# Two evacuations of stage 1 shared anew, and the drain before the MLP done group by group

**Chip, cores, metric.** One core of one Trainium2 chip. Times are device microseconds (us) of one execution. PE or TensorE multiplies matrices, ACT is ScalarE, DVE is VectorE and POOL is GpSimd.

## The reference, cut to what matters

The input has 2048 rows of 512. Two blocks follow each other, each with a layer norm and a residual:

```python
X  = rfft2(layernorm(x)) * (w_r + 1j * w_i)
h  = x + irfft2(X).astype(bf16)
a  = relu(layernorm(h) @ w1 + b1)
h2 = h + (a * a) @ w2 + b2
```

## The kernel before

The Fourier transforms are matmuls with tables of sines, which the kernel makes itself. It has these parts in time:

- **Stage 1** (to about 20 us): the 16 row groups of x are normalised and multiplied by a table. GpSimd makes the reciprocal roots of the variances (`rs1`), VectorE multiplies the table by them (the folds, `KFr`), TensorE multiplies, ScalarE or VectorE takes the result from PSUM to SBUF (the evacuation, `Bt`).
- **Spectral part** (to about 50 us): nine rounds with the intermediate tiles U, X (or AB, from which VectorE makes X), Z, M and T. `EI` is a table for the inverse transform: TensorE transposes it, ScalarE copies it from PSUM, VectorE negates parts of it (`EN`). `GI` and, with the change, `GIn` are tables of sines for the drain.
- **Drain** (50 to 57 us): the last inverse step for the first two row groups, their residual, second layer norm and transposes. Nothing of the MLP can start before it is through.
- **MLP** (57 us to the end): TensorE is busy; the matmuls into `ph` are its first half. The remaining row groups are drained beside it.

The parts that the change touches, cut:

```python
# stage 1. split=True: two PSUM tiles, evacuated in halves by ScalarE and VectorE
ln1_fold(6, 10)
angles_g(1)                       # two GpSimd instructions
ln1_rstd(10, 14)                  # add and power on GpSimd: the roots of groups 10 to 13
gathers = [w_reversed(0)]         # indirect DMA, made ready by GpSimd
...
nc.gpsimd.tensor_tensor(rs1[:, 14:16], rs1[:, 14:16], mhalf[:, 0:2], ALU.pow)
ln1_fold(12, 14)
gathers.append(w_reversed(1))
ln1_fold(14, 16)
stage1(10, cp=nc.vector.tensor_copy)
...
stage1(12)
tr08 = stage1(14, split=True, pre=lambda o: transposed(o, (0, 8), True))
# spectral rounds
for pr in range(9):
    ...
    if pr == 3:
        table_neg((4, 7))                         # VectorE, reads EI
        ...                                       # EN from EI, VectorE
    ...
    if pr == 1:
        table_neg((1, 3))
        tr = mm_tile("ptr", BF16)
        transposed(tr, (4, 5, 6, 7))              # TensorE
        table_i(tr, (4, 5, 6, 7))                 # ScalarE: EI
    if pr == 5:
        sin_of(GI[:].rearrange("p t c -> p (t c)"), fiI[:])    # ScalarE
# drain. s5: four matmuls into one bank, the odd half copied to od by ScalarE;
# s5b: R from sum and difference, VectorE; s6: matmul by KI; s6a/s6b: residual, statistics
s5(0); s5(1); s5(2, True); s5(3, True)
idle = bank("idle", "ph", 3)
s5b(0); s5b(1)
s6(0); s6b(0, True)
s6(1); s6a(1); s6b(1)
rstd(0); norm(0)
warm(idle[:], 12)                 # matmuls that do nothing but keep TensorE busy
s5b(2)
transp(0, 0); transp(0, 1)
for c in range(5):
    run(c)                        # the MLP
```

Of the kernel before, what the change touches and what calls it, by code (L numbers as in the profile page):

```python
# [34 lines left out]
def kernel(  # L35
# [43 lines left out]
    ones = persist.tile([P, 512], BF16, name="ones")  # L79
    KI = persist.tile([P, P], BF16, name="KI")  # L80
    GI = persist.tile([P, 4, 256], BF16, name="GI")
    T2 = persist.tile([P, 4, G, 16, 8], BF16, name="T2")

    fwd = tc.alloc_tile_pool(name="fwd", bufs=1)
# [34 lines left out]
    def mm_tile(name, dt=FP32):  # L119
        return ps.tile([P, 4096 // mybir.dt.size(dt)], dt, tag="mm", name=name)  # L120

    def sin_of(dst, fi):

        nc.scalar.activation(dst, fi.bitcast(I16)[:, ::2], ACT.Sin, scale=SIN_SCALE)
# [30 lines left out]
    def w_reversed(i):  # L155
        return nc.gpsimd.indirect_dma_start(
            out=WB[i][:, 9:16, :].rearrange("p j l -> p (j l)"), out_offset=None,
            in_=(A_w_r, A_w_i)[i].rearrange("k l -> (k l)").unsqueeze(1), element_offset=9 * Df,
            in_offset=bass.IndirectOffsetOnAxis(ap=idxR[:, 0:1], axis=0))
# [29 lines left out]

    nc.gpsimd.tensor_scalar(cols[:, 0:1], pF[:, 0:1], 128.0, None, ALU.mult)  # L190
    nc.gpsimd.tensor_scalar(cols[:, 1:2], pF[:, 0:1], 128.0, 16384.0, ALU.mult, ALU.add)

    def angles_g(t):
        o = 512 * t
        for r, q in ((0, QT), (256, HT)):
            nc.gpsimd.tensor_scalar(fiG[:, o + r:o + r + 256], idxL[:, r:r + 256], cols[:, t:t + 1], float(q),
                                    ALU.mult, ALU.add)

    def table_e(i):
        nc.scalar.activation(EF[:, :, i, :], fiE[i][:].bitcast(I16)[:, ::2].rearrange("p (a b) -> p a b", a=9),  # L200
# [25 lines left out]
    def ln1_rstd(a, b):  # L226
        nc.gpsimd.tensor_scalar(rs1[:, a:b], mv1[:, a:b, 1], EPS, None, ALU.add)
        nc.gpsimd.tensor_tensor(rs1[:, a:b], rs1[:, a:b], mhalf[:, 0:b - a], ALU.pow)
# [6 lines left out]
    def stage1(g0, n=0, split=False, pre=None, cp=nc.scalar.copy):  # L235
        if split:
            two = [mm_tile("p1a"), mm_tile("p1b")]
            pts = [pt[:, 0:512] for pt in two]
        else:
            pt = mm_tile("p1")  # L240
            pts = [pt[:, 0:512], pt[:, 512:1024]]
        pvs = [o.rearrange("p (e i c) -> p e i c", e=2, i=2) for o in pts]
        warm(pts[0], n)
        if pre:
            pre(two[0][:, 512:1024].bitcast(BF16))
        for t in range(2):
            for i in range(2):
                g = g0 + i
                o = pvs[t][:, :, i, :]
                nc.tensor.matmul(o, lhsT=xs[:, g, P * t:P * t + P],  # L250
                                 rhs=KFr[:, g, 0:P].unsqueeze(1).to_broadcast([P, 2, P]), start=True, stop=False)
                nc.tensor.matmul(o, lhsT=xs[:, g, 256 + P * t:256 + P * t + P],
                                 rhs=KFr[:, g, :].rearrange("p (e c) -> p e c", e=2), start=False, stop=True)
        dst = Bt[:].rearrange("p e q (g s) -> p e g q s", s=8)[:, :, g0:g0 + 2]
        if split:
            for t, cph in ((0, nc.scalar.copy), (1, nc.vector.tensor_copy)):
                cph(dst[:, 2 * t:2 * t + 2], pts[t].rearrange("p (e i q s) -> p e i q s", e=2, i=2, q=16))  # L257
            return two[0][:, 512:1024].bitcast(BF16)
        else:
            cp(dst, pt[:].rearrange("p (e i q s) -> p e i q s", e=4, i=2, q=16))  # L260

    def warm(o, n):

        for _ in range(n):
            nc.tensor.matmul(o, lhsT=ones[:, 0:P], rhs=ones[:], start=True, stop=True)  # L265
# [13 lines left out]
    def table_neg(ks):  # L279
        nc.vector.tensor_scalar(EI[:, ks[0]:ks[-1] + 1, 2, :], EI[:, ks[0]:ks[-1] + 1, 0, :], -1.0, None, ALU.mult)  # L280
# [29 lines left out]
    table_c(slice(0, 9, 8))  # L310
    ln1_stats(10, 12)
    ln1_fold(6, 10)
    angles_g(1)
    ln1_rstd(10, 14)
    gathers = [w_reversed(0)]
    stage1(6, 2)
    sin_of(GF[:].rearrange("p t c -> p (t c)"), fiG[:])
# [6 lines left out]
    ln1_fold(12, 14)  # L324
    gathers.append(w_reversed(1))
    ln1_fold(14, 16)
    stage1(10, cp=nc.vector.tensor_copy)
    for k, (dst, src) in enumerate(((W1[:], B_w1.rearrange("(c p) f -> p c f", p=P)),
                                    (W2[:], B_w2.rearrange("(i p) d -> p i d", p=P)),
                                    (b1b[:], B_b1.rearrange("(i p) -> p i", p=P)),  # L330
# [2 lines left out]
        if k == 0:  # L333
            for ga in gathers:
                after(load, ga, "the rows of W first")
    stage1(12)

    nc.vector.tensor_scalar(GF[:, :, 255:256], GF[:, :, 255:256], 0.5, None, ALU.mult)
    nc.vector.tensor_scalar(EF[:, :, 2, :], EF[:, :, 0, :], -1.0, None, ALU.mult)
# [169 lines left out]
    for pr in range(9):  # L509
        if pr == 1:  # L510
            stage3(3)
        if pr + 3 < 8:
            stage2(pr + 3)
        if pr == 0:
            tr = mm_tile("ptr", BF16)
            transposed(tr, (1, 2, 3))
            table_i(tr, (1, 2, 3))
        if 1 < pr and pr + 2 < 8:
            stage3(pr + 2)
        if pr == 7:  # L520
            warm(mm_tile("idle")[:, 0:512], 3)
        if pr > 0:
            stage4(pr - 1, split=(pr == 8))
        if pr == 8:
            warm(mm_tile("idle")[:, 0:512], 3)
        if pr == 3:
            table_neg((4, 7))
            nc.vector.tensor_scalar(EN[:].rearrange("p n (k b) -> p n k b", k=2), EI[:, NO_M[0]:NO_M[-1] + 1, 0:2, :],
                                    -1.0, None, ALU.mult)
        if pr == 0:  # L530
            spectral(0, first_tables)
        elif pr < 8:
            spectral(pr)
        if pr == 1:
            table_neg((1, 3))
            tr = mm_tile("ptr", BF16)
            transposed(tr, (4, 5, 6, 7))
            table_i(tr, (4, 5, 6, 7))
        if pr == 5:
            sin_of(GI[:].rearrange("p t c -> p (t c)"), fiI[:])  # L540
            nc.gpsimd.tensor_copy(b1f[:], b1b[:])
        if pr == 6:
            nc.scalar.activation(junk1[:], eps[:], ACT.Sqrt, bias=eps[:])
# [19 lines left out]
    def s5(g, ahead=False):  # L563
        pe = bank("p5", "po", 2) if ahead else bank("p5", "pp", 3)
        for e in range(2):
            for r in range(2):
                lt = 2 * r + e
                nc.tensor.matmul(pe[:, 256 - 256 * e:512 - 256 * e], lhsT=T2[:, lt, g].rearrange("p q s -> p (q s)"),  # L568
                                 rhs=GI[:, lt, :], start=(r == 0), stop=(r == 1))
        od = ffn.tile([P, 256], FP32, tag="od", bufs=4, name="od")  # L570
        nc.scalar.copy(od[:], pe[:, 256:512])  # L571
        Rs[g] = pe, od

    def s5b(g):
        pe, od = Rs[g]
        Rs[g] = R = ffn.tile([P, 512], BF16, tag="R", bufs=3, name="R")
        nc.vector.tensor_tensor(R[:, 0:256], pe[:, 0:256], od[:], ALU.add)  # L577
        nc.vector.tensor_tensor(R[:, 256:512], pe[:, 0:256], od[:], ALU.subtract)

    def s6(g):  # L580
        py = bank("p6", "pp", 3)
        if g == 0:
            nc.tensor.matmul(py[:], lhsT=identW[:], rhs=xs[:, 0, :], start=True, stop=False)
            nc.tensor.matmul(py[:], lhsT=KI[:], rhs=Rs.pop(g)[:], start=False, stop=True)
            nc.scalar.activation(hs[:, 0, :], py[:], ACT.Copy, scale=WSC, accum_out=mv2[:, 0, 0:1])
            return
        nc.tensor.matmul(py[:], lhsT=KI[:], rhs=Rs.pop(g)[:], start=True, stop=True)  # L587
        Ys[g] = py

    def s6a(g):  # L590
        nc.vector.scalar_tensor_tensor(hs[:, g, :], Ys.pop(g)[:], WSC, xs[:, g, :], ALU.mult, ALU.add)  # L591
# [20 lines left out]
    def rstd(c):  # L612
        a, b = CHUNKS[c]
        for par in range(2):
            mine = [g for g in range(a, b) if on_act(c, g) != bool(par)]
            if mine:
                st = mine[1] - mine[0] if len(mine) > 1 else 1
                sl = slice(mine[0], mine[-1] + 1, st)
                nc.scalar.activation(sd2[:, sl], mv2[:, sl, 1], ACT.Sqrt, bias=eps[:], scale=1.0 if par else float(D) ** -3 if c == 0 else 1.0 / D)
        if c == 0:  # L620
            nc.vector.tensor_scalar(mv2[:, 0, 0:1], mv2[:, 0, 0:1], 1.0 / D, None, ALU.mult)
        nc.vector.reciprocal(rs2[:, a:b], sd2[:, a:b])
# [4 lines left out]
    def norm(c):  # L627
        a, b = CHUNKS[c]
        us[c] = u2 = ffn.tile([P, 4, D], BF16, tag="u2", bufs=2, name="u2")
        for g in range(a, b):  # L630
            nc.vector.tensor_scalar(u2[:, g - a, :], hs[:, g, :], mv2[:, g, 0:1], rs2[:, g:g + 1],
                                    ALU.subtract, ALU.mult)
# [114 lines left out]
                piece()  # L747
                at += cost

    s5(0)  # L750
    s5(1)
    s5(2, True)
    s5(3, True)
    idle = bank("idle", "ph", 3)
    s5b(0)
    s5b(1)
    s6(0)
    s6b(0, True)
    s6(1)
    s6a(1)  # L760
    s6b(1)
    rstd(0)
    norm(0)
    warm(idle[:], 12)
    s5b(2)
    transp(0, 0)
    transp(0, 1)
    for c in range(5):
        run(c)
    pin(tc, nc)  # L770
# [30 lines left out]
```

## Time and profile before

| | before |
|---|---|
| time, median | 173.03 us |
| profiled span | 171.1 us |
| TensorE busy | 92% of the span |
| last evacuation of stage 1 starts (`Bt` from `p1b`) | 19.71 us |
| last T evacuation ends (the spectral part's end) | 49.92 us |
| group 1's matmul by `KI` starts | 52.70 us |
| first matmul into `ph` starts | 57.13 us |

A line of a timeline or of the chain has the start in us from the beginning of the span, the duration in us, the engine and what it did; a timeline adds the idle time before it and, behind an arrow, what ended that. TensorE is busy for 92% of the span, yet the part before 57 us is set by waits of one engine for another. The lines themselves are in the prediction.

### The profile page before, as it was taken

How to read it: one execution, taken by the hardware profiler on the slowest of the kernel's cores; microseconds unless marked ns; L12 is line 12 of the kernel's file. 1: busy time of each engine (PE TensorE's matmuls, PEld its weight loads, DVE VectorE, ACT ScalarE, POOL GpSimd, SP SyncE). 2: the span in 40 equal slices, each digit the busy share in tenths (PEclk: the TensorE clock that was granted, in tenths of full speed). 3: DMA queues.
4: the chain of work that ended last, by engine and by line, in shares of the span. 5: the costliest groups of instructions: out<-in, count | busy, mean ns of one | idle time of the engine just before them, and what ended most of it. 6: DMA issues, size and time to landing. Idle time of an engine off the chain costs nothing.

```text
span 171.1 us, 2723 instructions
## 1 busy us (share of the span) xinstructions
PE 158.0 (92%) x982; PEld 93.0 (54%) x997; DVE 125.9 (74%) x294; ACT 106.7 (62%) x188; POOL 36.3 (21%) x63
## 2 busy tenths in 40 slices
PE   3978897999989899899999999999999999999992
PEld 1455665877853675466445444544544454566461
DVE  6998789899957699758997577498667567578321
ACT  3999587998977582288662677254377534478200
POOL 7788800000000002235000135000035200025000
PEclk9999999999999999999999999999999999999999
DMA  5970759910000000010001100001000001010011
GB/s 158 349 261 2 215 168 397 297 35 2 0 0 4 0 0 2 32 35 0 0 21 31 44 0 0 2 31 34 31 31 0 0 31 34 13 48 0 0 59 38
DMA packets 7918, 10.29 MB, mean 60 GB/s; under 512 B 2272, under 2 KB 6368, under 8 KB 7904
## 3 DMA queue, kind: packets, MB, share of 16 engines
q1 hardware_dynamic: 7744, 9.19, 16.6%
q0 software_dynamic: 160, 0.92, 1.8%
q8 instruction: 8, 0.13, 0.3%
q14 instruction: 6, 0.05, 0.1%
HBM read 8.01 MB, written 2.10 MB: 59 GB/s over the span
## 4 chain that ended last, share of the span: by engine, by line
PE 69%; DVE 19%; ACT 6%; issue 3%; POOL 1%; DVEq 0%; POOLq 0%; ACTq 0%
PE ph L688 29%; PE po L721 25%; DVE st L221 4%; PE p L568 3%; PE p L362 3%; PE p L643 2%; ACT U L379 2%; PE po L709 2%; DVE KFr L232 2%; PE p L587 1%; DVE hs L591 1%; DVE mA L437 1%; ACT X L409 1%; DVE mB L437 1%; DVE Z L442 1%
## 5 line engine op out<-in xcount | busy, mean ns | idle before, releaser
L688 PE MATMUL ph<-UT,W 128*128 128x384 bf16 (+2 forms) x278 | 49.8, 336 | 1.5 <-ACT UT L647 1.0
L691 ACT ACTIVATE rl<-ph,b1f 128x384 bf16<-128x384 f32 (+2 forms) x70 | 41.5, 602 | 14.2 <-PE ph L688 11.0
L721 PE MATMUL po<-W,act 128*128 128x512 bf16 x203 | 48.1, 379 | 0.4
L692 DVE TENSOR_TENSOR act<-rl 128x384 bf16<-128x384 bf16 (+2 forms) x70 | 34.2, 514 | 16.2 <-ACT rl L691 15.7
L695 POOL TENSOR_TENSOR hb<-hs,b2b 128x512 f32<-128x512 bf16 x16 | 18.4, 1151 | 102.6 <-DVE act L692 102.6
L688 PEld LDWEIGHTS <-W 128*128 128x128 bf16 x280 | 27.4, 98 | 22.7 <-issue 1.9
L721 PEld LDWEIGHTS <-act 128*128 128x128 bf16 x210 | 20.4, 98 | 21.8
L725 DVE TENSOR_TENSOR ot<-po,hb 128x512 bf16<-128x512 f32 x15 | 10.3, 688 | 9.3 <-PE po L721 8.0
L571 ACT COPY od<-p 128x256 f32<-128x256 f32 x16 | 5.9, 368 | 9.1 <-PE p L568 9.0
L647 ACT COPY UT<-p 128x768 bf16<-128x768 bf16 (+2 forms) x5 | 4.2, 841 | 10.8 <-PE p L643 10.8
L591 DVE SCALAR_TENSOR_TENSOR hs<-p,xs 128x512 bf16<-128x512 f32 x15 | 10.2, 683 | 0.8 <-PE p L587 0.5
L265 PE MATMUL p<-ones 128*128 128x512 bf16 x22 | 7.3, 476 | 2.9 <-POOL ones L152 2.9
L568 PE MATMUL p<-GI,T 128*128 128x256 bf16 x64 | 9.1, 272 | 0.6 <-DVE T L489 0.2
L265 PEld LDWEIGHTS <-ones 128*128 128x128 bf16 x41 | 4.4, 109 | 7.6 <-POOL ones L152 2.9
L602 ACT ACTIVATE junk<-hs 128x512 bf16<-128x512 bf16 x6 | 3.8, 630 | 7.6 <-DVE hs L591 7.6
L362 PE MATMUL p<-GF,Bt 128*128 128x256 bf16 x64 | 8.3, 273 | 0.0
L568 PEld LDWEIGHTS <-T 128*128 128x128 bf16 x64 | 6.2, 97 | 3.9 <-issue 0.9
L250 PE MATMUL p<-KFr,xs 128*128 128x256 bf16 x28 | 6.4, 273 | 2.0 <-DVE KFr L232 2.0
L577 DVE TENSOR_TENSOR R<-p,od 128x256 bf16<-128x256 f32 x16 | 6.6, 414 | 2.1 <-ACT od L571 2.1
L221 DVE BATCH_NORM_STATS2 st<-xs 128x6 f32<-128x512 bf16 x12 | 7.8, 676 | 0.0
L491 ACT CAST T<-p 128x1024 bf16<-128x1024 f32 x7 | 7.2, 1027 | 0.0
L362 PEld LDWEIGHTS <-Bt 128*128 128x128 bf16 x64 | 6.1, 98 | 1.4 <-DVE Bt L257 0.4
(173 smaller groups left out, 228.7 us busy)
## 6 DMA issues: line engine op xcount, KB each, us to landing
W<-in_B_w_dram SPq DMA_DIRECT2D x2, 1792.0 KB, 9.7
out_dram<-ot SPq DMA_DIRECT2D x15, 128.0 KB, 1.8
xs<-in_A_x_dram SPq DMA_DIRECT2D x3, 512.0 KB, 5.6
WB<-in_A_w_r_dram SPq DMA_DIRECT2D x1, 578.2 KB, 5.3
WB<-in_A_w_i_dram SPq DMA_DIRECT2D x1, 578.2 KB, 6.3
xs<-in_A_x_dram SPq DMA_DIRECT2D x2, 256.0 KB, 3.3
b2b<-in_B_b_dram SPq DMA_DIRECT2D x1, 128.0 KB, 8.9
out_dram<-ot SPq DMA_DIRECT2D x2, 64.0 KB, 1.5
```

The costliest lines, as they stand in the source:

```text
L221: nc.vector.bn_stats(st[:], xs[:, g, :])
L265: nc.tensor.matmul(o, lhsT=ones[:, 0:P], rhs=ones[:], start=True, stop=True)
L362: nc.tensor.matmul(puv[:, :, e, :], lhsT=Bt[:, 2 * t + 1 - e, 2 * pr + q, :], rhs=GFv[:, t, :, e, :], start=(t == 0), stop=(t == 1))
L491: nc.scalar.copy(dst, src[0])
L568: nc.tensor.matmul(pe[:, 256 - 256 * e:512 - 256 * e], lhsT=T2[:, lt, g].rearrange("p q s -> p (q s)"), rhs=GI[:, lt, :], start=(r == 0), ...
L591: nc.vector.scalar_tensor_tensor(hs[:, g, :], Ys.pop(g)[:], WSC, xs[:, g, :], ALU.mult, ALU.add)
L688: nc.tensor.matmul(ph[:, 0:n], lhsT=W1[:, d, bass.ts(f, P)], rhs=UT[:, d, 0:n], start=(d == 0), stop=(d == ND - 1))
L691: nc.scalar.activation(rl[:, 0:n], ph[:, 0:n], ACT.Relu, bias=b1f[:, f:f + 1], scale=1.0)
L692: sq = nc.vector.tensor_tensor(act[:, f, 0:n], rl[:, 0:n], rl[:, 0:n], ALU.mult)
L695: add = nc.gpsimd.tensor_tensor(hb[:, g, :], hs[:, g, :], b2b[:], ALU.add)
L721: nc.tensor.matmul(po[:], lhsT=act[:, f, bass.ts(i, P)], rhs=W2[:, f, :], start=(f == 0), stop=(f == NF - 1))
L725: nc.vector.tensor_tensor(ot[:], po[:], hb[:, g, :], ALU.add)
```

## The change

Its intent: the last evacuations of stage 1 are shared between ScalarE and VectorE, so that VectorE ends sooner. The drain is to have fewer steps in a row: the odd half of group 0 gets its own bank, so its copy can start after two matmuls; group 1 is summed and subtracted by eight matmuls with a negated table `GIn`, so that it needs no VectorE; norm and transposes go group by group. The later tables move one round on.

```diff
-    angles_g(1)
+    nc.gpsimd.tensor_scalar(fiG[:, 512:768], idxL[:, 0:256], cols[:, 1:2], float(QT), ALU.mult, ALU.add)
     ln1_rstd(10, 14)
+    nc.gpsimd.tensor_scalar(fiG[:, 768:1024], idxL[:, 256:512], cols[:, 1:2], float(HT), ALU.mult, ALU.add)
     gathers = [w_reversed(0)]
...
-    stage1(10, cp=nc.vector.tensor_copy)
+    stage1(10)
...
-    stage1(12)
+    stage1(12, split=True)
...
-        if pr == 3:
+        if pr == 4:
             table_neg((4, 7))
...
         if pr == 1:
             table_neg((1, 3))
+        if pr == 2:
             tr = mm_tile("ptr", BF16)
             transposed(tr, (4, 5, 6, 7))
...
         if pr == 5:
             sin_of(GI[:].rearrange("p t c -> p (t c)"), fiI[:])
+            nc.scalar.activation(GIn[:], ...[:, 0::2, :], ACT.Sin, scale=-SIN_SCALE)
...
+    def s5_first(g):
+        two = [bank("p5o", "ph", 3), bank("p5", "pp", 3)]
+        ...            # two matmuls into each bank; od copied from the first
+    def s5_whole(g):
+        ...            # two halves of four matmuls, GIn in the second; R copied by ScalarE
...
-    s5(0); s5(1); s5(2, True); s5(3, True)          # one call a line, joined here
-    s5b(0); s5b(1); s6(0); s6b(0, True); s6(1); s6a(1); s6b(1)
-    rstd(0); norm(0)
-    warm(idle[:], 12)
+    s5_first(0); s5_whole(1); s5b(0); s6(0); s6(1)
+    rest = [s5(2, True), s5(3, True)]
+    s6a(1); s6b(0, True); s6b(1)
+    warm(idle[:], 11)
+    for g in range(2):
+        nc.scalar.activation(sd2[:, g:g + 1], ..., ACT.Sqrt, ...)
+    for g in range(2):
+        nc.vector.reciprocal(rs2[:, g:g + 1], sd2[:, g:g + 1])
+        nc.vector.tensor_scalar(u2[:, g, :], ...)
+    for g, cp in ((0, nc.scalar.copy), (1, nc.vector.tensor_copy)):
+        ...            # four transposes of group g, copied to UT
+    for r in rest:
+        r()            # the od copies of groups 2 and 3
     s5b(2)
-    transp(0, 0); transp(0, 1)
```

More of the change, by code (lines that the diff above doesn't have):

```diff
@@ L81 @@
     GI = persist.tile([P, 4, 256], BF16, name="GI")
+    GIn = persist.tile([P, 2, 256], BF16, name="GIn")
     T2 = persist.tile([P, 4, G, 16, 8], BF16, name="T2")
@@ L191 @@
     nc.gpsimd.tensor_scalar(cols[:, 1:2], pF[:, 0:1], 128.0, 16384.0, ALU.mult, ALU.add)
-    def angles_g(t):
-        o = 512 * t
-        for r, q in ((0, QT), (256, HT)):
-            nc.gpsimd.tensor_scalar(fiG[:, o + r:o + r + 256], idxL[:, r:r + 256], cols[:, t:t + 1], float(q),
-                                    ALU.mult, ALU.add)
     def table_e(i):
@@ L540 @@
             sin_of(GI[:].rearrange("p t c -> p (t c)"), fiI[:])
+            nc.scalar.activation(GIn[:], fiI[:].bitcast(I16)[:, ::2].rearrange("p (t c) -> p t c", t=4)[:, 0::2, :],
+                                 ACT.Sin, scale=-SIN_SCALE)
             nc.gpsimd.tensor_copy(b1f[:], b1b[:])
@@ L569, in s5, with rest @@
                                  rhs=GI[:, lt, :], start=(r == 0), stop=(r == 1))
-        od = ffn.tile([P, 256], FP32, tag="od", bufs=4, name="od")
-        nc.scalar.copy(od[:], pe[:, 256:512])
-        Rs[g] = pe, od
+        def rest():
+            od = ffn.tile([P, 256], FP32, tag="od", bufs=4, name="od")
+            nc.scalar.copy(od[:], pe[:, 256:512])
+            Rs[g] = pe, od
+        if ahead:
+            return rest
+        rest()
+    def s5_first(g):
+        two = [bank("p5o", "ph", 3), bank("p5", "pp", 3)]
+        for e in range(2):
+            for r in range(2):
+                nc.tensor.matmul(two[e][:, 0:256], lhsT=T2[:, 2 * r + e, g].rearrange("p q s -> p (q s)"),
+                                 rhs=GI[:, 2 * r + e, :], start=(r == 0), stop=(r == 1))
+        od = ffn.tile([P, 256], FP32, tag="od", bufs=4, name="od")
+        nc.scalar.copy(od[:], two[0][:, 0:256])
+        Rs[g] = two[1], od
+    def s5_whole(g):
+        pe = bank("p5", "pp", 3)
+        for h in range(2):
+            for k, lt in enumerate((1, 3, 0, 2)):
+                nc.tensor.matmul(pe[:, 256 * h:256 * h + 256], lhsT=T2[:, lt, g].rearrange("p q s -> p (q s)"),
+                                 rhs=GIn[:, lt // 2, :] if h and k > 1 else GI[:, lt, :], start=(k == 0), stop=(k == 3))
+        Rs[g] = R = ffn.tile([P, 512], BF16, tag="R", bufs=3, name="R")
+        nc.scalar.copy(R[:], pe[:])
     def s5b(g):
@@ L748, in run @@
                 at += cost
-    s5(0)
-    s5(1)
-    s5(2, True)
-    s5(3, True)
+    u2 = ffn.tile([P, 4, D], BF16, tag="u2", bufs=2, name="u2")
+    UTs[0] = ffn.tile([P, ND, 512], BF16, tag="UT", bufs=2, name="UT")
+    s5_first(0)
+    s5_whole(1)
+    s5b(0)
+    s6(0)
+    s6(1)
+    rest = [s5(2, True), s5(3, True)]
     idle = bank("idle", "ph", 3)
-    s5b(0)
-    s5b(1)
-    s6(0)
+    s6a(1)
     s6b(0, True)
-    s6(1)
-    s6a(1)
     s6b(1)
-    rstd(0)
-    norm(0)
-    warm(idle[:], 12)
+    nc.vector.tensor_scalar(mv2[:, 0, 0:1], mv2[:, 0, 0:1], 1.0 / D, None, ALU.mult)
+    warm(idle[:], 11)
+    for g in range(2):
+        nc.scalar.activation(sd2[:, g:g + 1], mv2[:, g, 1:2], ACT.Sqrt, bias=eps[:], scale=1.0 if g else float(D) ** -3)
+    for g in range(2):
+        nc.vector.reciprocal(rs2[:, g:g + 1], sd2[:, g:g + 1])
+        nc.vector.tensor_scalar(u2[:, g, :], hs[:, g, :], mv2[:, g, 0:1], rs2[:, g:g + 1], ALU.subtract, ALU.mult)
+    for g, cp in ((0, nc.scalar.copy), (1, nc.vector.tensor_copy)):
+        pt = bank("p7", "pp", 3, BF16)
+        for d in range(ND):
+            nc.tensor.transpose(pt[:, P * d:P * d + P], u2[:, g, bass.ts(d, P)], ident[:])
+        cp(UTs[0][:, :, P * g:P * g + P], pt[:, 0:ND * P].rearrange("p (d c) -> p d c", d=ND))
+    for r in rest:
+        r()
     s5b(2)
-    transp(0, 0)
-    transp(0, 1)
     for c in range(5):
```

## The prediction

> **What bounds the kernel now.** I read the page first, then the chain of waits in order of time, then the timelines of ScalarE, VectorE and TensorE over 12 to 68 us, where the edits lie. The page puts 69% of the chain on TensorE, nearly all in the two MLP matmul lines after 57 us. The edits touch nothing after that but bank numbers, so the question is one number: when does the first MLP matmul (ph) start? Before, it starts at 57.13 us. The page's shares of the chain:
> ```profile
> PE 69%; DVE 19%; ACT 6%; issue 3%; POOL 1%; DVEq 0%; POOLq 0%; ACTq 0%
> ```
> From the chain of waits of before in order of time (start, duration, engine, tile, line):
> ```profile
> 49.23 0.70 DVE T L489
> 49.93 0.14 issue
> 50.07 0.61 PE p L568 x4
> 50.75 0.38 ACT od L571
> 51.22 0.42 DVE R L577
> 51.65 0.33 DVE R L578
> 51.98 0.33 DVE R L577
> 52.31 0.34 DVE R L578
> 52.70 0.40 PE p L587
> 53.12 0.70 DVE hs L591
> ...
> 55.32 0.74 DVE u L631 x2
> 56.11 0.36 PE p L643 x3
> 56.49 0.59 ACT UT L647
> 57.13 1.48 PE ph L688 x12
> ```
> This is the drain between the spectral part and the MLP: every stage waits for the one before, so whatever is cut from it is gained in full. Two R pairs stand one after the other on VectorE; only then may group 1 go through its matmul at 52.70. Before the drain, from 38.78 to 48.43, VectorE works without a gap. From the timelines of before, first ScalarE:
> ```profile
> 32.90 1.03 ACT L277 COPY EI<-ptr 128x1024 bf16<-128x1024 bf16 x1
> 33.81 1.04 ACT L379 CAST U<-p 128x1024 bf16<-128x1024 f32 x1
> 34.99 1.01 ACT L409 CAST X<-p 128x1024 bf16<-128x1024 f32 x1
> 35.89 1.02 ACT L491 CAST T<-p 128x1024 bf16<-128x1024 f32 x1
> 36.80 1.03 ACT L379 CAST U<-p 128x1024 bf16<-128x1024 f32 x1
> 37.70 1.04 ACT L418 CAST AB<-p 128x1024 bf16<-128x1024 f32 x1
> ```
> VectorE, with the idle time before an instruction and what ended it in brackets:
> ```profile
> 33.97 0.29 DVE L280 TENSOR_SCALAR EI<-EI 128x512 bf16<-128x512 bf16 x1 [0.66 <-ACT EI L277]
> ...
> 38.78 0.42 DVE L427 TENSOR_TENSOR X<-AB 128x512 bf16<-128x512 bf16 x1 [0.17 <-ACT AB L418]
> ```
> TensorE:
> ```profile
> 19.08 0.27 PE L250 MATMUL p1b<-KFr,xs 128*128 128x256 bf16 x1 [0.43 <-DVE Bt L260]
> ...
> 52.92 2.75 PE L265 MATMUL idle<-ones 128*128 128x512 bf16 x12
> ```
> To be seen: ScalarE runs one evacuation after another at 0.90 us each from 34.99, so an insertion there delays AB; VectorE waited for ScalarE's EI (0.66) and AB (0.17); and the 12 warm-up matmuls fill the drain's idle TensorE.
>
> **What the Trainium skill says.** "PSUM — Partial Sum Buffer", section "Terms": two engines on one PSUM bank at once is an error. I take that to be why the od copy, which needs only the two odd-half matmuls, waits for all four of its bank: 50.07 + 0.61 = 50.68, then od at 50.75. The trace agrees. "ScalarE: Activation LUTs", section "What ACT_TABLE_LOAD costs": 186 ns + 0.833 ns per element with immediate operands, back-to-back overlap 93 ns, a table load 1283 ns. The load shows as 1.28 us; the 1024-element sine as 1.09 against 1.04 from the formula, so about 0.62 to 0.65 for the new 512-element sine, some 0.53 between starts. "TensorE: Matmul & The Clock Gate", section "Wait — 56ns, not 53.3ns?": start to start 215.7 ns at 512 columns when warm. The trace has (2.75 - 0.38)/11 = 0.215, and 0.109 at 256 columns.
>
> **The change part by part.** The build of the changed kernel gives order, banks and which instruction each wait names; durations are from before.
>
> *Stage 1.* The second angles instruction on GpSimd goes behind the reciprocal root of groups 10 to 13, so that ends about 0.5 sooner (15.03 to 14.50), as do the folds of 10 to 13 (about 0.4). The root of 14 and 15 is held by the gather, which ends at 16.42 either way: it starts at 16.44 instead of 16.65 and the last fold ends at 17.68 instead of 17.89. ScalarE takes the whole of group 10/11 in its 0.84 idle; VectorE only half of 12/13: 0.69 instead of 1.15 to 1.22. It ends at 18.29 instead of 19.03. But the pool gives the next tile, p1a of 14/15, the very bank that this half leaves: its transposes, which ran at 17.76, now wait until 18.34. From transposes to p1b are 0.28 + 4 x 0.11 = 0.72 us in order on TensorE: p1b at 19.06, against 19.08. The removed wait of 0.43 comes back one tile earlier. Worth: 0.0.
>
> *Spectral part.* The transposes of the tables 4 to 7 and their copy go one round later, their negations with them. TensorE: 0.44 us moved, X's matmuls of that round end 0.45 sooner. ScalarE: the EI copy leaves the slot at 32.90. U takes it, then nothing is ready until X at 34.54 (0.6 idle); T 35.44, EI 36.35, U 37.26, AB 38.16 to 39.20, against 37.70 to 38.74. VectorE loses the wait at 33.31 but then meets the same wait for EI later, until 37.38, at about 36.26 of its own time: 1.1 idle. Negations, mA and mB end at 39.11 and X waits for AB: 39.24 instead of 38.78. From there VectorE has no slack up to the last evacuation of T: +0.46, its end at 50.38 instead of 49.92.
>
> *GIn.* One more sine, 0.53 between starts: T, table load and the last half of T on ScalarE end at about 50.22 instead of 49.69. Alone +0.30 against VectorE's old end; beside the +0.46 it is covered.
>
> *Drain.* Counted from the end of T (E). Before, group 1's matmul (52.70) is at E + 2.78. Now od waits for two matmuls: 0.22 sooner, at E + 0.61. R of group 0 at E + 1.06 to 1.82. Group 1 comes whole from eight matmuls of 0.109 behind the four: issued up to E + 1.35, done E + 1.62, copied by ScalarE (0.60) until E + 2.26, its matmul at E + 2.30. Gain 0.48. After that matmul the old path is 57.13 - 52.70 = 4.43. Now two of its steps are cut: group 0 is normalised as soon as its root is there, and the transposes' copies are per group: hs +0.42, statistics to +1.9, root +2.4, second norm done +3.15, transposes and copy of 0.42: ph at about +4.10. But TensorE stands in order: the matmul 0.215, eight of groups 2 and 3 0.875, eleven warm-ups 2.365: free at +3.455, when both norms are done. Then eight transposes 0.44, result 0.17, VectorE copy with its semaphores 0.5: ph at +4.57. Loss 0.14. The od copies of groups 2 and 3 (0.74) lie before the first rl, and are hidden.
>
> *Sum.* 0.0 + 0.46 - 0.48 + 0.14 = +0.12 us: 173.03 + 0.12 = 173.15. I set 173.1, as a change that somebody kept more probably has a small gain that I miss than a loss.
>
> **The rivals.** (1) The drain gains as intended and TensorE's warm-ups do not hold the transposes: -0.8 in the drain, with the spectral +0.46 gives 172.7, with only GIn's +0.30 gives 172.5. For: the author took one warm-up away, as if fitting them. Against: eight real matmuls (0.875) replace one warm-up (0.215) in the same stretch, which before had 0.29 to spare. (2) The later tables cost nothing, because the 0.66 that VectorE waited is gained: then 172.2 to 173.0. For: that wait is in the trace. Against: ScalarE, back to back from 34.99, is what both waits name, and it gets the copy back at a busier place. (3) The new waits add up: VectorE's R of group 2, now behind the copy of UT, ends about 0.25 before its matmul needs it. If that fails, TensorE stalls in the first MLP part and loses 0.3 more: 173.5. (4) TensorE idle 0.85 at 17.5 to 18.3 lets the clock fall; the clock row shows nines throughout and the pauses of 0.8 at 28.3 in before did no harm, so I give it little.
>
> **Range and chances.** All parts are tenths of a microsecond; 2% would be 3.46 us, nearly half of the 7.21 us between E and ph. Range 172.5 (rival 1) to 173.5 (rival 3). Faster 0.01, same 0.98, slower 0.01.
>
> **What would show it.** Right: p1b's first matmul still near 19.1, and transposes of p1a waiting for VectorE's Bt; VectorE idle about 1 us before the negations, at 36 to 37.4, X from AB near 39.2; last T half at 50.3 to 50.4; group 1's matmul 2.3 after it; no idle on TensorE between the warm-ups and the transposes; ph near 57.25. Wrong: p1b at 18.7 or earlier; X from AB at or before 38.8; a wait of the transposes for u with idle TensorE; ph before 56.8. It would also be wrong if the MLP from ph to the end is not the same 114 us within 0.1.

## The result, and the profile after

| | before | after |
|---|---|---|
| time, median of 4 runs (lowest to highest) | 173.03 (173.02 to 173.32) | 173.56 (173.55 to 173.81) |
| profiled span | 171.1 | 171.7 |
| last evacuation of stage 1 starts | 19.71 | 20.01 |
| X from AB | 38.78 | 39.55 |
| last T evacuation ends (E) | 49.92 | 50.70 |
| group 1's matmul | 52.70 = E + 2.78 | 52.99 = E + 2.29 |
| first `ph` matmul | 57.13 | 57.66 |

Ratios are the mean time of one kernel's fast runs over that of the other's of the same rounds, so not quite the ratio of the medians quoted. Here it is 1.003, with a 95% interval of 1.0012 to 1.0047. By the 2% rule that is "same", and the kernel is about half a microsecond slower.

`ph` came 0.53 later, and the span grew by 0.6. The time of each kernel's profiled run is 115.8 to 115.9 us more than the start of its first `ph` matmul; the one exception is named below. So the loss lies ahead of the MLP, and the start of `ph` can serve as the measure.

Differences from mark to mark: the last evacuation of stage 1 is +0.30 late; X from AB is +0.77, so the spectral part added 0.47; the way from E to group 1's matmul lost 0.49 of its length; the way from there to `ph` went from 4.43 to 4.67, +0.24. Their sum is +0.52.

The shares of the chain by engine, from the page of after:

```profile
PE 71%; DVE 16%; ACT 5%; issue 3%; POOL 2%; DVEq 0%; POOLq 0%; ACTq 0%
```

VectorE's share fell from 19% to 16% and TensorE's rose from 69% to 71%. The path moved to TensorE; it did not become shorter.

**Stage 1.** GpSimd's timeline, first before:

```profile
15.21 1.21 POOL L156 DMA_INDIRECT WB<-in_A_w_r_dram,idxR  x1 [0.19 <-issue]
16.65 0.72 POOL L323 TENSOR_TENSOR rs<-rs,mhalf 128x2 f32<-128x2 f32 x1 [0.22 <-DVE rs L322]
```

and after:

```profile
13.46 1.11 POOL L223 TENSOR_TENSOR rs<-rs,mhalf 128x4 f32<-128x4 f32 x1
14.67 0.57 POOL L310 TENSOR_SCALAR fiG<-idxL,cols 128x256 int32<-128x256 int32 x1
15.43 1.23 POOL L157 DMA_INDIRECT WB<-in_A_w_r_dram,idxR  x1 [0.19 <-issue]
16.68 0.74 POOL L319 TENSOR_TENSOR rs<-rs,mhalf 128x2 f32<-128x2 f32 x1
```

The root of groups 10 to 13 now comes earlier (before it started at 14.00), and the second angles instruction comes behind it. Ahead of the gather stand the same four instructions as before, but in the new order they take longer, and the gather starts at 15.43 instead of 15.21. The root of groups 14 and 15 stands directly behind the gather with no idle time: before, it waited 0.22 for VectorE's addition (16.39 to 16.56); after, that addition is through at 16.34, and the root waits for GpSimd's own queue. So it starts where it started before, although its input comes 0.22 earlier.

VectorE after, in stage 1 and in the spectral part:

```profile
17.90 0.69 DVE L252 CAST Bt<-p1b 128x512 bf16<-128x512 f32 x1
...
37.72 0.29 DVE L275 TENSOR_SCALAR EI<-EI 128x512 bf16<-128x512 bf16 x1 [1.17 <-ACT EI L272]
...
39.55 0.42 DVE L423 TENSOR_TENSOR X<-AB 128x512 bf16<-128x512 bf16 x1
```

TensorE after, in stage 1:

```profile
17.59 0.27 PE L247 MATMUL p1b<-KFr,xs 128*128 128x256 bf16 x1
18.65 0.40 PE L265 MATMUL p1a<-ident,EF 128*128 128x128 bf16 x4 [0.79 <-DVE Bt L252]
...
19.38 0.27 PE L245 MATMUL p1b<-KFr,xs 128*128 128x256 bf16 x1
```

VectorE's half evacuation (17.90) waits for two things that end almost together: the last folds (started at 17.46; VectorE goes on 0.40 after such a start in before) and the last matmul of groups 12 and 13, which ends at 17.59 + 0.27 = 17.86. It ends at 18.59. The transposes wait 0.79 for exactly that instruction, because their tile got the bank that it leaves. What before was a wait of 0.43 ahead of `p1b` is now a wait of 0.79 ahead of `p1a`, and `p1b` starts 0.30 later than before (19.08).

The folds of groups 10 and 11 start 0.45 earlier than before (14.61, before 15.06) but take 0.71 instead of 0.48, with the second angles instruction now running beside them on GpSimd. In all thirteen traces they take 0.71 in the new order and 0.48 in the old one; what slows them was not tried apart. So the folds of 12 and 13 start only 0.23 earlier (16.24), and their first matmul only 0.06 earlier (16.83, before 16.89).

**Spectral part.** ScalarE after:

```profile
34.84 1.01 ACT L405 CAST X<-p 128x1024 bf16<-128x1024 f32 x1 [0.60 <-PE p L403]
...
36.66 1.03 ACT L272 COPY EI<-ptr 128x1024 bf16<-128x1024 bf16 x1
...
38.47 1.05 ACT L414 CAST AB<-p 128x1024 bf16<-128x1024 f32 x1
...
45.97 0.65 ACT L538 ACTIVATE GIn<-fiI 128x512 bf16<-128x512 int16 x1
```

ScalarE has a hole of 0.60 where the EI copy was, and the copy now stands in the unbroken row behind it. AB starts at 38.47, against 37.70 before. VectorE's wait for EI grew from 0.66 to 1.17.

**Drain.** The chain of waits after, in order of time:

```profile
50.01 0.70 DVE T L485
...
50.84 0.39 PE p5o L583 x2
...
51.76 0.42 DVE R L602
52.19 0.34 DVE R L603
...
52.99 0.38 PE p L612
53.36 0.87 PE p L567 x8
...
54.29 2.32 PE idle L260 x10
56.61 0.46 PE p L798 x8
...
57.09 0.44 DVE UT L799
...
57.66 1.47 PE ph L713 x12
```

Only one pair of R is left in the chain. From 52.99 on it never leaves TensorE until the transposes are done: eight matmuls for groups 2 and 3, then warm-ups. In the timeline of VectorE the two normalised groups were written by 55.59 and 56.11, yet the transposes start at 56.45, behind the last warm-up. Warm-ups, meant to fill idle time, set the end.

### The profile page after: what moved, and what is told of

The parts are those of the page before. It is cut to its first block, busy times and chain, and to the rows that moved or that the text cites. A ratio compares the mean times of both kernels' runs of the same rounds, so it can differ in the third digit from the quotient of the medians.

```text
span 171.7 us, 2732 instructions
## 1 busy us (share of the span) xinstructions
PE 158.5 (92%) x986; PEld 93.3 (54%) x1000; DVE 124.9 (73%) x293; ACT 107.9 (63%) x190; POOL 36.5 (21%) x63
## 4 chain that ended last, share of the span: by engine, by line
PE 71%; DVE 16%; ACT 5%; issue 3%; POOL 2%; DVEq 0%; POOLq 0%; ACTq 0%
PE ph L713 28%; PE po L746 24%; DVE st L216 3%; PE p L567 3%; PE p L358 3%; ACT U L375 2%; PE po L734 2%; PE p L668 2%; PE p L612 1%; PE idle L260 1%; POOL rs L223 1%; DVE KFr L227 1%; DVE mA L433 1%; ACT X L405 1%; DVE mB L433 1%
## 5 line engine op out<-in xcount | busy, mean ns | idle before, releaser
L260 PE MATMUL p<-ones 128*128 128x512 bf16 x22 | 7.8, 501 | 2.9 <-POOL ones L153 2.9
L571 ACT COPY od<-p 128x256 f32<-128x256 f32 x14 | 5.1, 370 | 7.9 <-PE p L567 7.9
L672 ACT COPY UT<-p 128x768 bf16<-128x768 bf16 (+1 forms) x4 | 3.6, 906 | 9.4 <-PE p L668 9.4
L567 PE MATMUL p<-GI,T 128*128 128x256 bf16 x56 | 8.2, 272 | 0.4 <-DVE hs L616 0.4
L567 PEld LDWEIGHTS <-T 128*128 128x128 bf16 x56 | 5.5, 97 | 3.5 <-issue 1.2
L630 DVE BATCH_NORM_STATS2 st<-hs 128x6 f32<-128x512 bf16 x9 | 6.3, 695 | 0.3
```

Source lines behind the costliest of these rows:

```text
L260: nc.tensor.matmul(o, lhsT=ones[:, 0:P], rhs=ones[:], start=True, stop=True)
L567: nc.tensor.matmul(pe[:, 256 - 256 * e:512 - 256 * e], lhsT=T2[:, lt, g].rearrange("p q s -> p (q s)"), rhs=GI[:, lt, :], start=(r == 0), ...
```

## The experiments

**Theory A** is the sum above: four independent terms. Stage 1 costs 0.30 through gather, late root and the bank that `p1a` gets; the later tables with `GIn` cost 0.47; the first half of the drain gains 0.49; the warm-ups take 0.24 of it back. **The rivals (B)** differ by run and are told with it: that a wait was only the named one and the next comes last just after it; that an engine's slack is smaller than A counts; that the warm-ups are needed.

**How a tenth is read.** The start of the kernel is not the same in each run. The first such run, before with only the new drain, has on VectorE:

```profile
7.31 0.69 DVE L216 BATCH_NORM_STATS2 st<-xs 128x6 f32<-128x512 bf16 x1 [0.61 <-DMA xs<-in_A_x_dram]
```

In before and after there is no such wait for the load of x. Traces are therefore compared after taking off an offset: the start of the statistics of row group 6, which before and after have both at 8.63. It is 0.71 in that run and 0.00 to 0.53 in the others. Why the load comes later is open; the runs of before that were timed beside the experiments spread too, from 172.9 to 173.8, so the timed medians show tenths only loosely. Figures of `ph` that are predicted are without that offset. "Net" below means less the offset. The kernel after was timed in the first session only, so ratios are all to before.

### Undoing stage 1

```diff
+    nc.gpsimd.tensor_scalar(fiG[:, 768:1024], ...)
     ln1_rstd(10, 14)
-    nc.gpsimd.tensor_scalar(fiG[:, 768:1024], ...)
-    stage1(10)
+    stage1(10, cp=nc.vector.tensor_copy)
-    stage1(12, split=True)
+    stage1(12)
```

> The changed kernel with its stage-1 edits alone undone (evacuations and angles as in the kernel before). Theory A (the 0.30 us that the prediction missed were made in stage 1: the transposes wait for VectorE's half evacuation, restart late, and p1b's matmuls go from 19.08 to 19.54): the second p20 matmul back near 20.46, all later marks 0.30 earlier, 173.26 us. Rival B (the pool gives every later tile other banks, and the loss comes from those): stage 1 as in before but less than 0.1 us of gain, 173.5.

Measured: `ph` at 57.41, net 57.36, so 0.30 earlier than after. Time 173.47 (173.18 to 173.85), ratio to before 1.0012 (0.9994 to 1.0030). The edits of stage 1 together (sharing and order of the angles) cost 0.30, as A has it. The timed median shows less of it (173.26 was expected); the profiled run took 173.22.

### Moving the transposes of the first tables one tile earlier

They need nothing of the last folds. They go to the tile of groups 12 and 13, so that the tile of 14 and 15 has only its matmuls left behind the bank.

```diff
-    stage1(12, split=True)
+    tr08 = stage1(12, split=True, pre=lambda o: transposed(o, (0, 8), True))
-    tr08 = stage1(14, split=True, pre=lambda o: transposed(o, (0, 8), True))
+    stage1(14, split=True)
```

> The changed kernel with the five transposes of tables 0 and 8 and of KF moved from stage-1 tile 14/15 to tile 12/13, before its matmuls, where TensorE idles 0.64 us. Theory A (in the changed kernel TensorE stands at p1a until VectorE's half evacuation ends at 18.6 and then has transposes and eight matmuls to issue before p1b is done at 19.98): p1a's matmuls still restart near 18.65, p1b is done near 19.69, all later marks 0.29 earlier, 173.27 us. Rival B (the late last folds alone set p1b): unchanged, 173.56.

Measured: the last evacuation starts at 19.80, net 19.66, against 20.01 after; `ph` net 57.30, 0.36 earlier. Time 173.23 (173.09 to 173.44), ratio 1.0004 (0.9990 to 1.0019). The wait for the bank remains, 0.82 long, but 0.29 of work no longer stands behind it. This fits A, with 0.07 more than it said; the half evacuation too starts 0.05 earlier here (net 17.85).

### Putting the first gather behind the last root

```diff
-    gathers = [w_reversed(0)]
...
-    gathers.append(w_reversed(1))
+    gathers = [w_reversed(0), w_reversed(1)]
```

> The changed kernel with the first gather issued behind the reciprocal root of groups 14 and 15 on GpSimd. Theory A (in the changed kernel the gather holds that root from 16.34, when its input is there, to 16.68): the root starts near 16.4, the last folds near 17.15 instead of 17.46, VectorE's half evacuation and all after it 0.3 earlier, 173.26 us. Rival B (VectorE's half evacuation waits for the matmuls of tile 12/13, not for VectorE to be free): less than 0.1 us. Rival C (the later gather holds the first products with the gathered rows of W): slower.

Measured: the root starts at 16.51, net 16.41, and the last folds net 17.15 (after: 16.68 and 17.46). So it is the gather in GpSimd's queue that holds them in after. But `ph` is net 57.49, only 0.17 earlier, not 0.30. VectorE of this run, where the folds now end early:

```profile
17.83 0.69 DVE L252 CAST Bt<-p1b 128x512 bf16<-128x512 f32 x1
```

and TensorE:

```profile
17.52 0.27 PE L247 MATMUL p1b<-KFr,xs 128*128 128x256 bf16 x1
```

The matmul that completes the half of groups 12 and 13 ends at 17.52 + 0.27 = 17.79, and the evacuation starts 0.04 later, the same distance as in after: the next wait stood just behind the one taken away. B named this wait but expected less than 0.1, so the gain lies between the two. The last evacuation is net 19.85, still 0.14 later than before. Rival C has no support in this trace: nothing waits for the gathered rows. The timed runs show no gain at all: 173.81 (173.39 to 174.2), ratio 1.0040 (1.0024 to 1.0055), while its profiled run has 173.39. That is a miss for both theories, and what made the other runs longer was not found.

### Undoing only the order of the angles

```diff
+    nc.gpsimd.tensor_scalar(fiG[:, 768:1024], ...)
     ln1_rstd(10, 14)
-    nc.gpsimd.tensor_scalar(fiG[:, 768:1024], ...)
```

> The changed kernel with the order of the angles on GpSimd alone undone. Theory A (the earlier root of groups 10 to 13 is worth nothing, because the gather, and with it the root of 14 and 15, is pushed back by as much): last folds within 0.1 of 17.46 after correction for the arrival of the input, time 173.5 to 173.65. Rival B (the new order is what made stage 1 slower): the last folds at 17.2 or earlier, 173.3.

Measured: the last folds net 17.29, 0.17 earlier than after, but the half evacuation starts net 17.85 (after 17.90) since it waits for the matmuls of groups 12 and 13, whose roots are late again. The last evacuation is net 19.96 and `ph` net 57.61, both 0.05 earlier than after. Time 173.80 (173.54 to 174.22), ratio 1.0042 (1.0021 to 1.0063). A's mark for the folds (within 0.1 of 17.46) was missed, and so was its time; its conclusion stands by the trace. The order of the angles is worth 0.05 here: it trades the root of the last groups for that of the groups before them.

### Undoing the move of the tables

```diff
-        if pr == 4:
+        if pr == 3:
             table_neg((4, 7))
...
-        if pr == 2:
             tr = mm_tile("ptr", BF16)
```

> The changed kernel with tables 4 to 7 back in their earlier rounds. Theory A (the later tables cost VectorE 0.47 us, but the additional sine GIn then holds ScalarE's last T copy, which ends at 50.51 in the changed kernel, only 0.19 before VectorE's): X from AB near 39.08, VectorE's last T copy ends near 50.23, ScalarE's stays at about 50.5, so the drain starts only 0.19 us sooner: 173.37 us. Rival B (GIn has slack): the whole 0.47 comes back, 173.09. Rival C (the later tables cost nothing): 173.56.

Measured: `ph` net 57.40, 0.26 earlier (A said 0.19). Time 173.48 (173.21 to 174.02), ratio 1.0013 (0.9993 to 1.0033). The gain is not 0.47, since ScalarE now ends last, as its timeline shows:

```profile
50.20 0.59 ACT L484 CAST T<-p4a 128x512 bf16<-128x512 f32 x1
```

VectorE's half of T ends at 50.51 and this one at 50.79. Behind the tables, the new sine `GIn` on ScalarE is the next bound.

### The move of the tables alone, in the kernel before

```diff
-        if pr == 3:
+        if pr == 4:
             table_neg((4, 7))
...
+        if pr == 2:
             tr = mm_tile("ptr", BF16)
```

> The kernel before with tables 4 to 7 moved one round later and nothing else. Theory A: VectorE waits near 36.3 to 37.4 for the table copy, X from AB near 39.24 instead of 38.78, everything after 0.47 later, 173.50 us. Rival B (the move pays for itself where nothing else is changed): 173.03 or less.

Measured: X from AB net 39.25 and `ph` net 57.61, so +0.48 against before. VectorE waits 1.17 for EI, as in after. Time 173.67 (173.41 to 173.94), ratio 1.0027 (1.0010 to 1.0044). The later tables have a cost of their own, and it is the largest single loss.

### The new drain alone, in the kernel before

```diff
 # before, with the whole drain of the change and GIn,
 # but its stage 1 and its rounds of the tables
```

> The kernel before with the drain edits and GIn alone (stage 1 and tables as before). Theory A: GIn moves the end of the last T copy by +0.29 (ScalarE now ends last, near 50.2), group 1's matmul 2.29 us later (-0.49), from there to ph 4.67 instead of 4.43 (+0.24): 173.07 us. Rival B (the drain as intended is a gain of its own and GIn is free): 172.8 or less.

Measured: `ph` net 57.11, against 57.13 before. Time 173.14 (172.87 to 173.62), ratio 0.9987 (0.9970 to 1.0004). By the trace the part that the change is for is worth nothing as written; the interval leaves room for up to half a microsecond. With the extra sine ScalarE's half of T ends last, net 50.22, 0.30 later than E before; group 1's matmul is nevertheless 0.27 earlier than before (net 52.43), and from there to `ph` 0.25 is lost again.

### Eight warm-ups instead of eleven

```diff
-    warm(idle[:], 11)
+    warm(idle[:], 8)
```

> The changed kernel with 8 instead of 11 warm-up matmuls in the drain. Theory A (the warm-ups hold the transposes, whose inputs are ready at 55.6 and 56.1 while TensorE comes free at 56.45): transposes of the second group near 56.2, ph near 57.2, 173.1 us. Rival B (the norms or the copies hold them): unchanged, 173.56. Rival C (fewer warm-ups let TensorE's clock fall): the first ph matmuls take longer than 0.11 us each and the time is above 173.56.

Measured: the transposes start at 55.80 instead of 56.45, and `ph` at 57.18, 0.48 earlier than after, with no offset to take off. Time 172.99 (172.98 to 174.05), ratio 0.9999 (0.9976 to 1.0023). The warm-ups held the transposes.

### Tables back, and the sine of GI earlier

With the tables back, `GIn` binds (above). ScalarE has idle time at 26 us, so the other sine goes there.

```diff
     stage3(1)
+    sin_of(GI[:].rearrange("p t c -> p (t c)"), fiI[:])
     stage3(2)
...
         if pr == 5:
-            sin_of(GI[:].rearrange("p t c -> p (t c)"), fiI[:])
```

and the edit of "undoing the move of the tables".

> The changed kernel with tables 4 to 7 in their earlier rounds and the sine GI (not GIn) moved into ScalarE's idle time near 26.4. Theory A (with the earlier tables ScalarE's last T copy, late by GIn, is what starts the drain; with GI gone it ends near 49.7 and VectorE's at 50.23 is last): the whole 0.47 comes back, 173.09 us, 0.28 below the kernel with the earlier tables alone by its trace. Rival B (GI does not fit the idle 1.07 us and delays X and what follows): 173.4 or more.

Measured: `ph` net 57.19, 0.47 earlier, which is the whole loss of the spectral part. Time 173.20 (172.97 to 173.4), ratio 0.9998 (0.9983 to 1.0014). Fits A.

### All repairs together

The edits of the sections on transposes, gather, tables with GI, and eight warm-ups.

> All that the runs so far point to: the changed kernel with the transposes of tables 0 and 8 at tile 12/13 (-0.29), the gather behind the last root (-0.30), tables 4 to 7 in their earlier rounds with GI in ScalarE's idle time (-0.47), and 8 warm-up matmuls in the drain (-0.48). If the terms add: 173.56 - 1.54 = 172.02 us, against 173.03 of before. If the two stage-1 terms overlap (p1b waits for the last folds or TensorE, whichever is later): 172.3.

Measured: `ph` at 56.19, net 56.13: 1.00 earlier than before and 1.53 earlier than after. The four single gains add up to 0.36 + 0.17 + 0.47 + 0.48 = 1.48. Time 172.23 (171.93 to 172.49), ratio to before 0.9948 (0.9933 to 0.9963). It beats before by about half a per cent; by the 2% rule this too is "same".

### The same without warm-ups

```diff
-    warm(idle[:], 8)
+    warm(idle[:], 0)
```

> The best kernel so far with no warm-up matmul in the drain at all. Theory A (8 are already too few to hold the transposes, and TensorE idling some 1.7 us there does not change its clock): ph at the same distance from the last T, ph's matmuls still 0.11 us apart, time as with 8, 172.0 us. Rival B (the idle time lets the clock fall): the transposes, or the ph matmuls after them, start more than 0.11 us apart for some time, and the time is 172.5 or more.

Measured: times 173.12, 173.3, 171.94 and 172.55, ratio 0.9970 (0.9933 to 1.0007). In the profiled run TensorE was idle for 1.41 before the transposes:

```profile
54.62 0.92 PE L796 MATMUL p<-ident,u 128*128 128x128 bf16 x8 [1.41 <-DVE u L792]
56.15 2.40 PE L711 MATMUL ph<-UT,W 128*128 128x256 bf16 x12 [0.61 <-DVE UT L797]
```

`ph` starts as early as in the run before, at 56.15, but the first twelve `ph` matmuls take 2.40 instead of the 1.47 that the chain of after shows. The table of stretches of 2 us tells why (its columns: the stretch, its length, the busy time of PE, PEld, DVE, ACT and POOL with the number of instructions in brackets, the granted clock of TensorE, the DMA share, GB/s):

```profile
56.00:58.00 2.00, 1.85 (x11) 1.42 (x12) 0.99 (x4) 0.93 (x3) 0.00 (x0) 0.63 0.00 0
58.00:60.00 2.00, 2.00 (x11) 1.28 (x10) 1.20 (x5) 0.81 (x3) 0.00 (x0) 0.52 0.00 0
```

The granted clock is 0.63 and 0.52 there; with eight warm-ups it is 1.00 in the same stretches. Asked by single microseconds, the trace gives 0.76, 0.50, 0.50 and 0.53, then 1.00: one fall to a half that lasted about 3 us. This is the exception named above: 116.97 us from `ph` to the end of the timed run instead of 115.8. The mean granted clock was 0.99 in the two slowest of the four runs and 0.999 and 1.00 in the other two (171.94 and 172.55), so the fall does not come in every run. Here B was right for the profiled run: some warm-ups are needed to be safe from this fall; the number is what must fit. Over all timed runs the ratios with eight and with none do not stand clearly apart.

## Why the prediction was right or wrong

The time came out at 173.56, just above the range of 172.5 to 173.5; "within 2%" was right. The question that it chose, when the first `ph` matmul starts, was the right one, though its reading of the page was off: the two MLP lines hold 29% + 25% of the 69% on TensorE, not nearly all of it.

- **Stage 1: wrong, and the part that failed.** The prediction said that the whole is "Worth: 0.0", with `p1b` at 19.06; it came at 19.38. Two of its terms failed. The first: the gather "ends at 16.42 either way"; it ended at 16.66. The prediction took two angles, an addition and a root to need the same time in either order. In the new order they took 0.22 more: the root 1.11 instead of 1.02, the addition 0.30 instead of 0.27, and the angles, which stood back to back before, now have pauses of 0.09 and 0.10 on their inner sides. All thirteen traces show it, each with its own order: 1.10 or 1.11 for this root in the new order, 1.02 or 1.03 in the old one. Why the root takes longer there was not tried. The last root then started at 16.68 instead of 16.44. The second: the folds of groups 10 to 13 come "about 0.4" sooner. Those of 12 and 13 came 0.23 sooner and their matmuls only 0.06, so these held the half evacuation too, a wait that the prediction did not count. It ended at 18.59 instead of 18.29. From there the prediction's mechanism holds: bank, transposes, 0.73 to `p1b`. Undoing stage 1 gave 0.30 back. With the gather out of the way the root started at net 16.41, near the 16.44 predicted, yet the half evacuation at net 17.73 instead of the 17.60 that the prediction implies: by the last evacuation, 0.16 of the 0.30 went with the gather and 0.14 stayed.
- **Spectral part: right.** Predicted +0.46, measured +0.47, and +0.48 when tried alone. The wait of 1.1 for EI was 1.17. X from AB was late by the 0.30 of stage 1 beside it.
- **GIn: right.** Start to start 0.51 against 0.53 predicted, and hidden behind VectorE; undoing the tables uncovered it.
- **First half of the drain: right.** Predicted gain 0.48, measured 0.49.
- **Second half of the drain: right in kind, too small.** Predicted +0.14, measured +0.24. Transposes started 3.46 after group 1's matmul (3.455 predicted). From transposes to `ph` took 1.21, not 1.11: the term "VectorE copy with its semaphores 0.5" measured 0.60, namely 0.03 ahead of the copy, 0.44 for it and 0.13 behind.
- **The sum.** Stage 1 accounts for 0.30 and the copy for 0.10 of the 0.40 between the +0.12 of the prediction and the +0.52 measured. The prediction also set 173.1 where its sum was 173.15, in trust that somebody had kept the change for a reason; nothing in the profile spoke for that.
- **Signs.** Most of what was to show it right came: transposes of `p1a` waiting for VectorE (0.79), the wait of 1.17, group 1's matmul 2.29 after E, no idle time ahead of the transposes. `p1b` at 19.38 was neither "near 19.1" nor at 18.7.
- **Rivals.** (1) Warm-ups that do not hold the transposes: false; three fewer gained 0.48. (2) Later tables that cost nothing: false; alone they cost 0.48. (3) A stall by R of group 2: no such stall; from `ph` on, the time did not change. (4) A clock that falls in stage 1: the clock row of after shows nines throughout. The top of the range rested on (3) alone, so it left no room for an error in the terms themselves.

## What to carry to other kernels

When an instruction is moved behind another in an engine's queue, look again at everything that stands behind it in that queue, even what is not in the diff: the same instructions in another order need not take the same time, and an instruction that had slack (here the last root, 0.22) can lose it. When one wait is taken away, ask what ends next: here a second wait stood 0.04 from the first, and nearly half of the 0.30 stayed with it. Warm-up matmuls stand in the queue like any others; fit their number to the time that is idle, and neither leave the old number when the path gets shorter nor take them all away. An instruction moved from a place where its engine then only idles (ScalarE, 0.60) to one where the engine has no idle time costs there what it did not cost before (here 0.47).

## What the Trainium skill lacked or had wrong

- "TensorE: Matmul & The Clock Gate", section "What's actually happening": its table puts the fall back to the lower clock after at least one idle window of about 3.4 us. Here the granted clock fell to a half with no idle time of TensorE longer than 1.41 us between 49 and 60 us, around sparse transposes, and two of four runs of the same kernel kept a mean clock of 0.999 or more. A later section of the page, "A second HAM failure mode: psum-queue depth-cycling", does say that frequent short idle times can do it, but not how much work in a window is enough; eight warm-ups of 0.215 us each were, in the runs here.
- "ScalarE: Activation LUTs", section "What ACT_TABLE_LOAD costs": an estimate from the formula (1.04 for 1024 elements, 0.61 for 512) fits the plain copies (0.99 to 1.08 and 0.58 to 0.62 here). The sines of every second int16 took a little more: 1.06 to 1.09 for 1024, which hardly stands out, and 0.65 to 0.67 for 512, which does. No run here tells whether the function or the input makes the difference.
- No page has GpSimd's power of a few numbers: 1.02 to 1.12 us for 128x4 and 0.70 to 0.74 us for 128x2 in fp32, nor the time that GpSimd takes to make an indirect gather ready, 0.95 to 1.23 us here (a first-byte time is given only for DMAs from GpSimd in general). Both bear on the end of stage 1.
